# Sixteen half rows of one key transfer, loaded four rows at a time

## The chip, the core and the metric

The kernel runs on one core of a Trainium2 chip. The core has five engines that work at the same time and meet at semaphores: TensorE (PE in the profile; PEld is its loading of weights), VectorE (DVE), ScalarE (ACT), GpSimd (POOL) and SyncE (SP). Data comes from the chip's memory through 16 DMA engines, which work through queues of transfers. Here SyncE issues all transfers. The metric is the time of one execution on the device in microseconds, and the number given for a kernel is the median of its runs.

## The reference

Two layers of a decoder, each for one new token of two sequences (B = 2, D = 576). A layer is attention over a stored cache of keys and values (32 heads, 16384 positions, 128 numbers each, in bf16), and then an MLP.

```
q = (layernorm(x) @ wq) by heads                   # 2 x 32 rows of 128
p = softmax(q . K^T / sqrt(128))                    # over 16384 positions
x = x + concat(p . V) @ wo
y = layernorm(x)
x1 = y + shift(gelu(layernorm(y) @ w1)) @ w2        # shift: along a sequence of length 1
x = x + x1 + gelu(layernorm(x1) @ w3) @ w4
```

Both layers use the same caches and the same weights. K and V of one head (of one sequence) are 4 MB each, and there are 64 such heads. That is 512 MB a layer, and all of it is read once a layer, less a few heads that stay on the chip from one layer to the next.

## The kernel before, in words

**Units and places.** Heads are numbered u = 0 to 63. One tensor `mem` holds six places of 32 KB a row in 128 rows. A single head's K or V fills one place. Most heads go in pairs: K of heads u and u+1 is one block of 128 rows of 65536 bytes (names `kp`), rows 0 to 63 of the first head, the others of the second. V of a pair is loaded alike (`vp`). K of pairs alternates between two double places, V has one double place. The first layer goes through one single head, 30 pairs and three single heads; the second begins with those last three, whose K it finds on the chip, and goes on with 30 pairs and one single head.

**Transfers.** `plan_all` writes down all transfers in order, by `plan_pair`, `plan_tile` and others. Each entry has a name, a semaphore, a place and a list of starts, each with a destination and a source. `Store.pump` issues the entries strictly in this order on SyncE, each as soon as all of its place has been released, every start of an entry as a DMA of its own. An entry at the head of the list that has no place yet holds all behind it. A pair can be loaded in pieces (`cuts`, in blocks of 128 numbers of a row): pair 1 of the second layer, heads 0 and 1, comes in five, four of 8 KB a row and then the one of 32 KB a row, blocks 0 to 127. Its starts count on the semaphore `part0_0`.

**Work on a pair.** For blocks 0 to 127, `pair_transposes` (L1395) turns eight blocks at a time with TensorE, ScalarE copies them out (`evacuate`, L1496), and `pair_scores` (L1406) multiplies them with q. For blocks 128 to 255, `pair_dots` does it on VectorE (L1418, L1421). `pair_max` and `pair_exp` make the softmax, and `pair_exp` ends with a ScalarE instruction (L1460) that waits until K is no longer used; then K's place is free. In the middle of the next pair's blocks TensorE multiplies p with V (`pv_pair_part`, L1473, 256 matmuls), and ScalarE keeps the sum (`keep_pair`, L1482), after which V's place is free. The next V transfer waits for this one.

**Relays.** Landings are told to TensorE and VectorE through GpSimd (L206), which waits for the transfers' semaphores one after another in program order and counts up a semaphore of the waiting engine. `shared` and `landed` put these relays into the program.

**Between the layers.** After the last three heads come `wo`, the MLP, the second layer's `wq` (L951, L825, L843) in small transfers through a ring of places, and then the first heads of the second layer from what is on the chip (`carried`: L1506 scores, L1592 sums over V). During this the first pieces of pairs 1 and 2 of the second layer are loaded. Their issues wait for the last uses of the places.

Of the kernel before, what the change touches and what calls it, by code (L numbers as in the profile page):

```python
# [342 lines left out]
class KB:  # L343
# [117 lines left out]

        return (self.K if t == "k" else self.V)[u // self.H, u % self.H].rearrange("(p j) d -> p (j d)", p=128)

    def plan_pair(self, t, u, slot, cuts=()):

        v = (self.K if t == "kp" else self.V).rearrange("b h s d -> (b h s d)")
        n = self.NB * 128 * 128
        src = v[u * n:(u + 2) * n].rearrange("(p x) -> p x", p=128)
        for a, z in cuts or [(0, 2 * self.NB)]:
            sem = f"pair{slot}" if z - a == 2 * self.NB else f"part{slot}_{a}"  # L470
            self.store.plan((t, u, a, z - a), sem, slot * self.TILE + 256 * a, 256 * (z - a),
                            [(lambda m: m, src[:, a * 128:z * 128])])

    def plan_piece(self, t, u, base, src, a, n):
# [70 lines left out]
    def cols4(self, l, buf, m):  # L545
# [3 lines left out]
        base = 0 if buf.shape[1] == 128 * self.MT else m // half * half  # L549
        return buf[:, (lo - base) * 128 + m - lo:(hi - base) * 128:hi - lo]  # L550

    def plan_small(self, nm, l, w, at, cuts):
        D, KT, TL = self.D, self.KT, self.TL
        self.store.plan((nm, l), nm, at, 2 * KT * D, [
            ((lambda m: m[:, 0:(KT - 1) * D]), w[0:(KT - 1) * 128, :].rearrange("(p k) n -> p (k n)", p=128))] + [
            ((lambda m, a=a, b=b: m[TL + a:TL + b, (KT - 1) * D:KT * D]), w[(KT - 1) * 128 + a:(KT - 1) * 128 + b, :])
            for a, b in zip(cuts[:-1], cuts[1:])])

    def plan_all(self):

        T, U, n = self.TILE, self.U, self.KT - 1
        row, w3r, wqr = 2 * self.D, 2 * self.F, 2 * 128 * self.H
        H, MT = self.H, self.MT
        self.parts = {}
        self.plan_cols("wq", 0, self.wq, self.whole(self.wq, [4 * T, None, None, None, 4 * T + 4 * wqr]))
        self.plan_small("w2", 0, self.w2, 4 * T + wqr * n + wqr // 2, (0, 64))

        half, quarter = self.BP, self.BP // 2
        self.plan_tile("k", 0, 2)
        self.plan_tile("v", 0, 3)  # L570
        o, n = self.order(0), self.PAIRS[0]
        place = lambda i: 0 if i % 2 else 2
        self.plan_pair("kp", o[1], place(1), [(2 * half, 4 * half), (0, 2 * half)])
        for i in range(2, n + 1):
            self.plan_pair("kp", o[2 * i - 1], place(i))
            self.plan_pair("vp", o[2 * i - 3], 4)
        a, b, c = o[2 * n + 1:]
        self.plan_tile("k", a, 1)
        self.plan_tile("k", b, 0)
        self.plan_pair("vp", o[2 * n - 1], 4)  # L580
        self.plan_tile("v", a, 2)
        self.plan_tile("k", c, 3)
        self.plan_tile("v", b, 4)
        self.plan_tile("v", c, 5, self.LATE[1:-1])

        self.cuts = {}
        P = 4 * row
        ring = [3 * T - 256 * self.GONE + P * i for i in range(6)]
        assert ring[-1] + P <= 3 * T + 256 * 8 * self.PARKED
        turn = iter([ring[i] for i in (0, 2, 3, 1, 4, 5)] * 6)  # L590
        h = MT // 2
        self.cuts["wo", 0] = [(i, i + 4, next(turn)) for i in range(0, 32, 4)]
        halves = lambda n: [(k, m, z, next(turn)) for k in range(self.KT - 1) for m, z in ((0, n), (n, 2 * n))] + \
                           [(self.KT - 1, 0, 2 * n, next(turn))]
        w3 = halves(h)
        g = (0, 4, 8, 12, 16, 18)
        self.groups = [(g, g), ((0, 12, 16, 18), (0, 8, 12, 16, 18))]
        self.cuts["w4", 0] = [(h * i + p, h * i + q, next(turn)) for i in range(2) for p, q in zip(g[:-1], g[1:])]
        self.plan_rows("wo", 0, self.wo, self.cuts["wo", 0])
        self.plan_cols("w3", 0, self.w3, w3)  # L600
        self.plan_groups("w4", 0, self.w4, self.cuts["w4", 0])
        self.plan_cols("wq", 1, self.wq, halves(H // 2))

        kept = self.NB - self.GONE
        again = lambda i, z: self.plan_piece("v", U - 3, 2 * T, self.rows_of("v", U - 3), i, z - i)
        again(kept, kept + 18)
        o, n = self.order(1), self.PAIRS[1]
        early = [(2 * half + i, 2 * half + i + self.DB) for i in range(0, self.EARLY, self.DB)]
        self.plan_pair("kp", o[5], place(2), early[:1])
        again(kept + 18, self.NB - self.SPARE - self.LENT)  # L610
        self.plan_pair("kp", o[5], place(2), early[1:])
        self.plan_pair("kp", o[3], place(1), [(quarter * i, quarter * (i + 1)) for i in range(4, 8)] + [(0, 2 * half)])
        for i in range(2, n + 1):
            self.plan_pair("kp", o[2 * i + 1], place(i), [(0, 2 * half), (2 * half + self.EARLY, 4 * half)] if i == 2 else ())
            self.plan_pair("vp", o[2 * i - 1], 4)
        self.plan_tile("k", o[-1], 0)
        self.plan_tile("v", o[-1], 1)
        self.plan_pair("vp", o[2 * n + 1], 4, [(0, 2 * half), (2 * half, 4 * half)])
        at = 2 * T
        self.cuts["wo", 1] = [(i, j, at + i * row) for i, j in ((0, 32),)]  # L620
        at += 32 * row
        ats = [at, None, None, 0, w3r]
        assert at + 3 * w3r <= 4 * T
        w4_at = w3r + w3r // 2
        self.cuts["w4", 1] = [(a, b, w4_at + a * row) for a, b in ((0, 12), (12, 18), (18, 26), (26, 30), (30, 34), (34, 36))]
        w1_at = w4_at + 36 * row
        assert w1_at + 5 * row <= 2 * T
        self.plan_rows("wo", 1, self.wo, self.cuts["wo", 1])
        self.plan_cols("w3", 1, self.w3, self.whole(self.w3, ats))
        self.plan_groups("w4", 1, self.w4, self.cuts["w4", 1])  # L630
        n = self.KT - 1
        self.store.plan(("w1", 1, 0), "w1_0", w1_at, n * row, [
            (lambda m: m, self.w1[0:128 * n, :].rearrange("(p k) n -> p (k n)", p=128))])
        self.store.plan(("w1", 1, 1), "w1_1", w1_at + 4 * row, row, [(lambda m: m[self.TL:, :], self.w1[4 * 128:, :])])
# [789 lines left out]
    def halves(self):  # L1424

        return [(h, slice(64 * h, 64 * h + 64)) for h in range(2)]
# [267 lines left out]
```

## Time and profile before

| | |
|---|---|
| median of 3 runs | 2537.85 us (2537.55 to 2538.87) |
| the profiled execution | 2539.74 us, span of its instructions 2538.0 us |
| read from memory | 1090.93 MB |
| busy, PE / PEld / DVE / ACT / POOL | 64% / 58% / 74% / 49% / 1% |

The span is the time from the first to the last instruction of the profile; the execution's own time is 1.7 us longer. A share of busy time is a mean over stages with different limits. In the parts below, a number that stands behind L is a line of the kernel before. In the windows view, a DMA share or a rate counts the packets that start in a window, so in a window shorter than a packet it can be far over 1, or 0. "issue" as the end of a wait is time in which an engine waited for nothing that the profile shows.

### The profile page before, as it was taken

To read this page: it belongs to the slowest core of one execution; us is meant where nothing else is said; L and a number is where in the kernel's file an instruction comes from. 1 tells how busy PE (TensorE), PEld (TensorE's weight loads), DVE (VectorE), ACT (ScalarE), POOL (GpSimd) and SP (SyncE) were. 2 spreads that over 40 slices of the span, in tenths; PEclk is the share of its full clock that TensorE was granted. 3 is DMA by queue.
4 is the path that set the end of the run, shared out by engine and by line. 5 is a ranking of instruction groups with operands and counts; after the bars stand their busy time and mean duration, and the time that the engine had idled before them with its cause. 6 is when DMAs were issued, how large, how long until landed. Compare 5 with 4: busy or idle time off the path is not lost.

```text
span 2538.0 us, 82125 instructions
## 1 busy us (share of the span) xinstructions
PE 1626.1 (64%) x34346; PEld 1483.1 (58%) x34346; DVE 1883.8 (74%) x1559; ACT 1252.9 (49%) x1940; POOL 31.3 (1%) x95
## 2 busy tenths in 40 slices
PE   3666665666666566657767665666566566656666
PEld 3555665665566556556666655565566556555656
DVE  5877787787787777777658877877778778778773
ACT  2545545445446455455435564454554544644542
POOL 0000000000000000000000000000000000000000
PEclk8666666666666666666656666666666666666665
DMA  9999999999999999999999999999999999999999
GB/s 415 432 435 432 433 434 434 433 433 435 434 433 434 434 433 434 434 433 432 415 407 413 438 437 430 430 431 444 431 430 431 440 435 430 430 436 440 430 430 388
DMA packets 28305, 1091.78 MB, mean 430 GB/s; under 512 B 3156, under 2 KB 3288, under 8 KB 9816
## 3 DMA queue, kind: packets, MB, share of 16 engines
q1 hardware_dynamic: 28248, 1090.95, 99.8%
q8 instruction: 45, 0.74, 0.1%
q14 instruction: 12, 0.10, 0.0%
HBM read 1090.93 MB, written 0.00 MB: 430 GB/s over the span
## 4 chain that ended last, share of the span: by engine, by line
DMA 77%; PE 18%; issue 3%; ACT 2%; DVE 0%; SPq 0%; ACTq 0%; POOLq 0%; POOL 0%; DVEq 0%
DMA mem<-in_A_v_cache_dram 72%; PE mps L1473 15%; DMA mem<-in_A_wo_dram 2%; DMA mem<-in_B_w_dram 1%; DMA mem<-in_A_k_cache_dram 1%; ACT kt L1496 1%; PE mps L1592 1%; ACT o_acc L1482 0%; PE mps L951 0%; PE tps L1395 0%; DMA mem<-in_A_wq_dram 0%; PE tps L1380 0%; PE mps L1506 0%; PE tps L1506 0%; ACT both L1451 0%
## 5 line engine op out<-in xcount | busy, mean ns | idle before, releaser
L1395 PE MATMUL tps<-same,mem 128*128 128x128 bf16 x7680 | 950.5, 267 | 254.4 <-POOLq L206 252.7
L1421 DVE TENSOR_REDUCE s_dve<-prod 128x16 f32<-128x2048 bf16 x480 | 1097.4, 2286 | 16.5
L1496 ACT ACTIVATE kt<-tps 128x1024 bf16<-128x1024 bf16 x985 | 991.5, 1026 | 198.6 <-PE tps L1395 176.8
L1395 PEld LDWEIGHTS tps<-same,mem 128*128 (+1 forms) x7680 | 707.3, 112 | 364.8 <-issue 254.4
L1418 DVE TENSOR_TENSOR prod<-mem,qb 128x2048 bf16<-128x2048 bf16 x480 | 588.0, 1225 | 344.4 <-POOLq L206 280.7
L1473 PE MATMUL mps<-both,mem 128*128 128x2 bf16 x15360 | 420.1, 165 | 437.0 <-POOLq L206 423.6
L1473 PEld LDWEIGHTS mps<-both,mem 128*128 128x128 bf16 x15360 | 414.8, 103 | 442.6 <-POOLq L206 428.9
L1482 ACT ACTIVATE o_acc<-mps 128x2 f32 (+1 forms) x59 | 10.2, 173 | 794.2 <-PE mps L1473 794.2
L1406 PE MATMUL sps<-q_pair,kt 128*128 128x2 bf16 x7680 | 347.9, 167 | 50.2 <-ACT kt L1496 47.4
L1406 PEld LDWEIGHTS sps<-q_pair,kt 128*128 128x128 bf16 x7680 | 328.3, 104 | 62.0 <-ACT kt L1496 61.4
L1437 DVE TENSOR_REDUCE mq<-sps 64x1 f32<-64x128 f32 x120 | 34.6, 289 | 166.0 <-PE sps L1406 164.1
L1342 ACT ACTIVATE qb<-sps 128x128 bf16<-128x128 f32 x66 | 18.3, 277 | 139.4 <-PE sps L1338 139.4
L1338 PE MATMUL sps<-same,q_pair 128*64 128x128 bf16 x120 | 17.8, 293 | 80.3 <-DVE q_pair L1351 76.8
L1338 PEld LDWEIGHTS sps<-same,q_pair 128*64 128x64 bf16 x120 | 7.5, 121 | 85.5 <-DVE q_pair L1351 82.0
L1520 DVE TENSOR_REDUCE s_dve<-prod 128x16 f32<-128x2048 bf16 x24 | 54.9, 2286 | 0.8
L1380 PE MATMUL tps<-same,mem 128*128 128x128 bf16 x432 | 45.0, 277 | 7.3 <-POOLq L206 4.4
L1442 POOL PARTITION_ALL_REDUCE mq<-mq x60 | 21.4, 357 | 2268.8 <-DVE mq L1440 2268.8
L1451 ACT ACTIVATE both<-s_dve,mq 64x128 bf16<-64x128 f32 x120 | 47.9, 399 | 2.3
L1517 DVE TENSOR_TENSOR prod<-mem,qb 128x2048 bf16<-128x2048 bf16 x24 | 29.4, 1224 | 22.1 <-DMA mem<-in_A_k_cache_dram 12.5
L1455 ACT ACTIVATE both<-sps,mq 64x128 bf16<-64x128 f32 x120 | 43.5, 363 | 3.0
L1380 PEld LDWEIGHTS tps<-same,mem 128*128 128x128 bf16 x432 | 36.6, 127 | 8.1 <-POOLq L206 4.9
L1592 PE MATMUL mps<-p,mem 128*128 128x1 bf16 x888 | 25.8, 165 | 20.7 <-ACT p L1549 10.2
(163 smaller groups left out, 462.7 us busy)
## 6 DMA issues: line engine op xcount, KB each, us to landing
mem<-in_A_k_cache_dram SPq DMA_DIRECT2D x9, 4096.0 KB, 30.0
mem<-in_A_v_cache_dram SPq DMA_DIRECT2D x6, 4096.0 KB, 30.8
mem<-in_B_w_dram SPq DMA_DIRECT2D x23, 576.0 KB, 7.7
mem<-in_A_wq_dram SPq DMA_DIRECT2D x10, 512.0 KB, 6.5
mem<-in_A_wo_dram SPq DMA_DIRECT2D x8, 576.0 KB, 13.0
mem<-in_A_wo_dram SPq DMA_DIRECT2D x1, 4608.0 KB, 31.6
mem<-in_A_wq_dram SPq DMA_DIRECT2D x1, 4096.0 KB, 12.8
mem<-in_A_k_cache_dram SPq DMA_DIRECT2D x4, 1024.0 KB, 9.6
```

The lines of the kernel that those rows point to most:

```text
L1380: ins = pe.transpose(to[:, j * 128:(j + 1) * 128], buf[:, j * 128:(j + 1) * 128], self.ident[:, :])
L1395: ins = pe.transpose(self.tps[t][:, j * 128:(j + 1) * 128], self.mem[:, bass.ds(base + (c * self.CH + j) * 128, 128)], self.ident[:, :])
L1406: ins = pe.matmul(self.sps[1][:, i:i + 2], lhsT=buf[:, j * 128:(j + 1) * 128], rhs=self.q_pair[:, :], start=True, stop=True, skip_group_ch ...
L1418: self.dv(lambda e, base: e.tensor_tensor(out=prod, in0=self.mem[:, bass.ds(base + b * 128, DB * 128)].rearrange("p (j d) -> p j d", d=128 ...
L1421: self.dv(lambda e: e.tensor_reduce(out=self.s_dve[2][:, d * DB:(d + 1) * DB], in_=prod, axis=AX.X, op=ALU.add), reads=["prod"], writes=[( ...
L1437: self.dv(lambda e, h=h, r=r: e.tensor_reduce(out=m[r, 1:2], in_=self.pair_scored(r, h), axis=AX.X, op=ALU.max), reads=[("sps", 1)], write ...
L1451: self.act(lambda e, h=h, r=r: e.activation(out=self.both[r, h, n:2 * n], in_=self.s_dve[2][r, :], func=ACT.Exp, bias=m[r, 6:7], scale=sel ...
L1455: self.act(lambda e, h=h, r=r: e.activation(out=self.both[r, h, 0:n], in_=self.pair_scored(r, h), func=ACT.Exp, bias=m[r, 6:7], scale=self ...
L1473: ins = pe.matmul(self.mps[:, 448:450], lhsT=buf[:, at:at + 128], rhs=self.both[:, :, b], start=b == 0, stop=b == 2 * self.NB - 1, skip_gr ...
L1496: self.act(lambda e: e.activation(out=out, in_=src, func=ACT.Copy), reads=[key], writes=keys, sig=("evac", key, keys[0]))
L1520: self.dv(lambda e: e.tensor_reduce(out=self.s_dve[z][:, d * DB:(d + 1) * DB], in_=prod, axis=AX.X, op=ALU.add), reads=["prod"], writes=[( ...
L1592: ins = pe.matmul(out, lhsT=buf[:, j * 128:(j + 1) * 128], rhs=p[:, b:b + 1], start=b == 0, stop=b == self.NB - 1, skip_group_check=True)
```

## The change

`plan_pair` gets an argument `tilt`. The piece that begins at block `tilt` is no longer one transfer of 128 rows. `tilted` divides it: rows 0 to 111 as whole rows (32 KB each), the right halves of rows 112 to 127 (16 rows of 16 KB), and their left halves in four transfers of four rows (16 KB a row). It is used once, for blocks 0 to 127 of pair 1 of the second layer. All six count on the same semaphore, so whoever waits for the piece waits for all six. The bytes and their places stay the same.

```diff
-    def plan_pair(self, t, u, slot, cuts=()):
+    def plan_pair(self, t, u, slot, cuts=(), tilt=None):
...
             self.store.plan((t, u, a, z - a), sem, slot * self.TILE + 256 * a, 256 * (z - a),
+                            self.tilted(lambda m: m, src[:, a * 128:z * 128], (z - a) * 64) if a == tilt else
                             [(lambda m: m, src[:, a * 128:z * 128])])
...
+    @staticmethod
+    def tilted(to, src, cut):
+
+        lo, hi = slice(0, cut), slice(cut, src.shape[1])
+        spots = [(slice(0, 112), slice(0, src.shape[1])), (slice(112, 128), hi)]
+        spots += [(slice(p, p + 4), lo) for p in range(112, 128, 4)]
+        return [(lambda m, p=p, c=c: to(m)[p, c], src[p, c]) for p, c in spots]
...
-        self.plan_pair("kp", o[3], place(1), [(quarter * i, quarter * (i + 1)) for i in range(4, 8)] + [(0, 2 * half)])
+        self.plan_pair("kp", o[3], place(1), [(quarter * i, quarter * (i + 1)) for i in range(4, 8)] + [(0, 2 * half)], 0)
```

SyncE's transfers between the layers, before and now (rows x numbers of two bytes; the four of 128x4096 are pair 1's first pieces, 128x10240 belongs to pair 2):

```order
 L101 DMA mem<-in_A_k_cache_dram 128x2048 x2
 L101 DMA mem<-in_A_k_cache_dram 128x4096 x4
-L101 DMA mem<-in_A_k_cache_dram 128x16384 x2
+L101 DMA mem<-in_A_k_cache_dram 112x16384
+L101 DMA mem<-in_A_k_cache_dram 16x8192
+L101 DMA mem<-in_A_k_cache_dram 4x8192 x4
+L101 DMA mem<-in_A_k_cache_dram 128x16384
 L101 DMA mem<-in_A_k_cache_dram 128x10240
 L101 DMA mem<-in_A_v_cache_dram 128x32768
```

The first of the two transfers of 128x16384 has become six; the second, pair 2's, stands behind them as before. On the other four engines the instructions and their order are the same. The one wait for the piece is GpSimd's, before its first maximum of the second layer's pairs (the row with `part0_0`), and what stands around it has not moved:

```order
L1535 ISA mx<-mx 128x1 [waits piece2_84_18,piece2_102_10,part0_224,part0_192,part0_128,part0_160,done_vector]
L1286 MEMSET both 128x512
L1442 ISA mq<-mq 128x2 [waits part0_0,done_vector]
L1442 ISA mq<-mq 128x2 [waits part2_0,part2_176,part2_160,part2_128,part2_144,pair4,done_vector]
L1442 ISA mq<-mq 128x2 [waits pair0,pair4,done_vector]
```

These are the rows of before; in the changed kernel only their line numbers are nine higher.

## The prediction

> **What bounds the kernel now.** I read the page first, parts 2 to 4 and the chain of waits.
>
> ```profile
> GB/s 415 432 435 432 433 434 434 433 433 435 434 433 434 434 433 434 434 433 432 415 407 413 438 437 430 430 431 444 431 430 431 440 435 430 430 436 440 430 430 388
> ...
> q1 hardware_dynamic: 28248, 1090.95, 99.8%
> ...
> DMA 77%; PE 18%; issue 3%; ACT 2%; DVE 0%; SPq 0%; ACTq 0%; POOLq 0%; POOL 0%; DVEq 0%
> ```
>
> The 16 DMA engines are busy 99.8% of the span, at some 434 GB/s in nearly every slice, or 434 / 16 = 27.1 GB/s an engine. Every byte is loaded once, so the time is the bytes of one engine over 27.1 GB/s, plus what an engine idles, plus how far the last engine is behind the others at the end. The change leaves the bytes as they are. It can act on the other two alone. The slices below 430 (415, 407, 413, from 1206 to 1396 us) hold the passage between the layers, where the changed transfer lies. There I read the issues of the DMA queue in order of time, and from the view of DMA issues the time to landing of each.
>
> ```profile
> 1319.09 7.78 SPq L101 DMA_DIRECT2D mem<-in_A_k_cache_dram  x3
> 1344.09 0.33 SPq L101 DMA_DIRECT2D mem<-in_A_v_cache_dram  x1
> 1367.24 0.33 SPq L101 DMA_DIRECT2D mem<-in_A_k_cache_dram  x1
> 1389.95 0.33 SPq L101 DMA_DIRECT2D mem<-in_A_v_cache_dram  x1
> 1401.13 0.33 SPq L101 DMA_DIRECT2D mem<-in_A_k_cache_dram  x1
> ```
> ```profile
> mem<-in_A_k_cache_dram SPq DMA_DIRECT2D x1, 4096.0 KB, 16.7
> ...
> mem<-in_A_v_cache_dram SPq DMA_DIRECT2D x1, 28.2
> ...
> mem<-in_A_k_cache_dram SPq DMA_DIRECT2D x1, 24.6
> ```
>
> The 4096 KB issue at 1319.09 is the one that the change divides. It lands 16.7 us later, at 1335.8. The V of 1344.09 lands at 1372.3, the K of 1367.24 at 1391.8. The V of 1389.95 is issued 1.9 us before that K is in, so the queue nearly runs out. The windows view around it shows that it does (the last two columns are the busy share of the 16 DMA engines and GB/s, by packets that start in the window):
>
> ```profile
> 1387.50:1388.00 0.50, 0.50 (x23) 0.50 (x22) 0.50 (x1) 0.00 (x0) 0.00 (x0) 0.50 0.30 131
> 1388.00:1388.50 0.50, 0.50 (x25) 0.50 (x23) 0.47 (x2) 0.00 (x0) 0.00 (x0) 0.50 0.00 0
> 1388.50:1389.00 0.50, 0.50 (x25) 0.50 (x23) 0.50 (x1) 0.00 (x0) 0.00 (x0) 0.50 0.61 262
> 1389.00:1389.40 0.40, 0.40 (x22) 0.40 (x19) 0.40 (x1) 0.00 (x0) 0.00 (x0) 0.50 0.38 164
> 1389.40:1390.90 1.50, 1.50 (x30) 1.50 (x27) 1.36 (x2) 0.52 (x2) 0.00 (x0) 0.50 0.05 11
> 1390.90:1391.20 0.30, 0.30 (x6) 0.30 (x4) 0.30 (x1) 0.30 (x1) 0.00 (x0) 0.50 8.32 2840
> 1391.20:1391.50 0.30, 0.30 (x7) 0.30 (x6) 0.30 (x1) 0.30 (x1) 0.00 (x0) 0.50 1.83 655
> ...
> DMA packets 239, 13.57 MB, mean 433 GB/s; under 512 B 32, under 2 KB 32, under 8 KB 32
> ```
>
> The last row is the DMA view of a later stretch, 1420.5 to 1451.8: 207 packets over 512 B carry 13.57 MB, 65.5 KB each, which is a whole row of a pair. So a row is one packet, and a packet of 65.5 KB takes 65.5 / 27.1 = 2.42 us of its engine. Now the windows can be counted: 1 packet starts from 1387.5 to 1388.0 (131 GB/s x 0.5 us), none until 1388.5, 2 + 1 until 1389.4, then no data (16 KB of code) until 1390.9. There 13 start within 0.3 us (2840 x 0.3 / 65.5) and 3 more by 1391.5. So 13 engines were through by 1388.0 + 2.42 = 1390.4, 12 of them by 1389.9, and stood empty. Only 3 had data until 1390.9 to 1391.8. The 16 engines start again side by side at 1390.9, 0.96 us after the issue of 1389.95. **What one engine was behind another before that is mostly wiped out there.** What sets 1389.95 is TensorE, by its timeline and by SyncE's waits:
>
> ```profile
> 1343.92 2.72 PE L1395 MATMUL tps<-same,mem 128*128 128x128 bf16 x24
> ...
> 1363.93 3.26 PE L1395 MATMUL tps<-same,mem 128*128 128x128 bf16 x24
> ...
> 1377.11 1.44 PE L1473 MATMUL mps<-both,mem 128*128 128x2 bf16 x49
> ...
> 1387.39 2.25 PE L1473 MATMUL mps<-both,mem 128*128 128x2 bf16 x79 [3.74 <-issue]
> ```
> ```profile
> SPq L101 <- ACT o_acc L1482: 22.4, 1, 22.4
> ...
> PE mps L1473 <- issue: 5.3, 2, 3.7
> ```
>
> Pair 1 of the second layer starts at 1343.92, pair 2 at 1363.93; the sums over V start at 1377.11, in program order, 4.8 us after their V (1372.3). They stop twice, 5.3 us, for no data, and ScalarE's copy after them (L1482) lets the queue go on. The end shows what is at stake there: the last weight transfer is issued at 2513.65, and its landing releases the last matmuls.
>
> ```profile
> 2534.50:2535.00 0.50, 0.47 (x9) 0.23 (x5) 0.00 (x0) 0.07 (x1) 0.00 (x0) 0.50 0.08 16
> 2535.00:2535.50 0.50, 0.00 (x0) 0.00 (x0) 0.48 (x1) 0.31 (x1) 0.00 (x0) 0.50 0.06 18
> 2535.50:2536.00 0.50, 0.00 (x0) 0.00 (x0) 0.00 (x0) 0.00 (x0) 0.00 (x0) 0.50 0.05 18
> ...
> 2513.65 22.55 DMA mem<-in_B_w_dram
> ```
>
> A share of 0.06 is one engine of 16: from about 2535.0 to the landing at 2536.2 a single engine works, 1.2 us behind all others.
>
> **The change part by part.**
>
> *Issues.* One issue becomes six. An issue takes 0.33 us in the view of the issuing line:
>
> ```profile
> L101 SPq DMA_DIRECT2D mem<-in_A_k_cache_dram x74: 327/328/580, 3.1 to 2438.0; - x74
> ```
>
> Five more are 5 x 0.33 = 1.6 us, 2.9 at the slowest of the row. SyncE is then done by 1322.3; in the row of three issues that begins at 1319.09 it otherwise waits for TensorE, the last issue of that row ending at 1319.09 + 7.78 = 1326.87. The queue has work meanwhile, since the divided piece itself lands only 16.7 us after its issue. Without that cover it would be 1.6 us; with it 0.
>
> *Bytes of an engine.* 128 rows of 32 KB are 8 rows an engine, 256 KB. Now each engine gets 7 rows (112 rows) and half a row (the 16 right halves): 240 KB, 16 KB less, or 16.4 / 27.1 = 0.60 us. The left halves are 16 rows of 16 KB in four transfers. A row is one packet, so a transfer of four rows works on four engines at most. No row of before shows such a transfer, so I bound it: if they fall on all 16 engines alike, nothing changes; if all four fall on the same four engines, these have 240 + 64 = 304 KB, 48 KB more, 49.2 / 27.1 = **1.81 us later**, and the other twelve 0.60 us earlier; if all fall on a single engine, it gets 256 KB above the 240. I take the middle one, as four rows with one packet each are nearest to four engines.
>
> [...]
>
> *The waits behind it.* The landing moves from 1335.8 to between 1335.2 and 1337.6; pair 1 reads it from 1343.92, which leaves 6 us. The next K pieces, also up to 1.81 later, are read from 1363.93. V moves from 1372.3 to 1374.1 at most, against 1377.11. So TensorE and the issue at 1389.95 stay where they are; if the 4.8 us of cover were gone, the 1.81 would be paid in full.
>
> *The restart.* Twelve engines were through by 1389.9. One of these with 1.81 us more is through by 1391.7, 0.3 us after the last start seen there (1391.5, less than that for most). One of the other four ends 1.8 us later than now. The earlier ones gain nothing but idle time. From then on each engine has the same bytes as before, and the spread is carried to the end.
>
> *Sum* on the profiled execution (2539.74 us, with a span of 2538.0 and 1.7 us around it): issues 0, bytes 0 in all, TensorE 0, the four engines 0 to +0.3, of which I take +0.2: 2539.9. That execution lies 1.9 us over the median of the runs (2537.85, from 2537.55 to 2538.87); on the median, **2538.05 us**.
>
> **The rivals.**
>
> *The four engines stay last (+1.8).* If one of them is among the three that had data until 1390.9 or later, it starts V up to 1.8 us after the rest and keeps that to the end: 2539.7. For it: 3 of 16 engines were late, and four are loaded. Against it: the end is already set by a single engine 1.2 us behind, so a second engine has to pass that one first.
>
> *The end gets more even (-0.6 to -1.2).* If the engine that is last is one of the twelve and keeps its 0.60 us, or swaps its place with a loaded one, the last landing comes up to 1.2 us sooner: 2536.7. Against it: the restart lies between.
>
> *One engine takes the half rows (slower).* If the four-row transfers are not divided over engines at all, one engine carries 240 + 16 x 16 = 496 KB in place of 256; 240 KB more are 245.8 / 27.1 = 9.1 us. It ends at about 1390.4 + 9.1 = 1399.5 in place of starting V at 1390.9; V lands last on it, and the end moves by 8.6 us: 2546.4. It decides from 0.5 us of such a surplus on, which is what the empty engines had. Against it: the row-per-packet count above.
>
> *Each small transfer costs a pause (slower).* From issue to first packet the restart took 0.96 us; five more such pauses, if nothing overlapped, are 4.8 us. V would land at 1377.1, just as it is read, and the engines end at up to 1395.2 in place of 1390.9: +4.3, 2542.2. Against it stands the window from 1256 to 1290, where transfers of 576 KB follow one another:
>
> ```profile
> q1 hardware_dynamic: 3361, 13.47, 100.0%
> ...
> mem<-in_B_w_dram SPq DMA_DIRECT2D x17, 576.0 KB, 7.4
> ```
>
> with no share lost. [...]
>
> *TensorE's stops move (either sign).* Its two stops of 5.3 us before 1389.95 are not for data. If they lengthen by as much again, the restart and the end move by +5.3 to 2543.2; if they vanish, -5.3.
>
> **How the numbers follow.** A measurement of this kernel can tell about 0.2%, 5.1 us, from no change. Forecast 0.67; four engines last 0.15; a more even end 0.09; one engine 0.02; pauses 0.03, half of it past 5.1 us; TensorE's stops 0.04, half of it to each side. Faster has the 0.02 of shorter stops; slower 0.02 of one engine, 0.015 of the pauses and 0.015 of longer stops, 0.05; the rest is same, 0.93. The range starts at the lowest run less what a more even end could bring (2537.55 - 1.2 - 0.6 = 2535.75) and ends at the highest run with four engines last and the 0.3 us of the restart (2538.87 + 1.81 + 0.3 = 2541.0). The cases outside hold under 0.1.
>
> **What would show it.** Right: six issues in a row from 1319.1, with the next big K issue still about 1326; TensorE's L1395 at about 1343.9 and 1363.9; the V issue near 1390.0; windows after it in which the engines start within a microsecond of each other; the same 434 GB/s until the end. Wrong: windows near 1390 in which some engines start V two or more microseconds after the rest while the end moves with them (four engines, or one); a share under 1 between 1326 and 1340 (pauses); a V issue away from 1390 by microseconds, with TensorE's stops before it changed.

## The result and the profile after

| | before | after |
|---|---|---|
| median | 2538.01 us (6 runs, 2537.55 to 2538.87) | 2551.77 us (6 runs, 2551.36 to 2552.26) |
| the profiled execution | 2539.74 us, span 2538.0 | 2552.04 us, span 2550.2 |

The ratio is 1.0054, with a 95% interval of 1.0041 to 1.0067: 13.8 us slower. The prediction said 2538.05 us and no change, with a range up to 2541.0. It was wrong, by 13.7 us.

The page of the changed kernel, parts 2 and 4, shows where, but hardly what:

```profile
DMA  9999999999999999999999999999999999999999
GB/s 413 433 432 435 433 434 434 434 434 433 434 434 433 433 435 434 432 434 434 410 366 378 436 430 436 435 431 435 434 433 433 434 434 433 434 433 436 431 431 390
...
DMA 75%; PE 19%; issue 3%; ACT 2%; DVE 1%; SPq 0%; ACTq 0%; POOLq 0%; POOL 0%; DVEq 0%
```

Two slices of 64 us have lost speed, 407 and 413 GB/s before and 366 and 378 now, and the others are within 3% of what they were. The DMA engines are shown as busy throughout, in those slices too: they did not idle, they were slow. The windows view says how slow (the last two columns: busy share of the 16 engines, GB/s), first for the changed kernel, then for the kernel before:

```profile
1326.00:1338.00 12.00, 4.02 (x127) 3.72 (x128) 10.18 (x10) 2.49 (x5) 1.71 (x2) 0.50 1.01 242
1338.00:1350.00 12.00, 3.71 (x128) 3.54 (x127) 11.76 (x8) 1.29 (x7) 0.00 (x0) 0.50 0.99 138
1350.00:1354.00 4.00, 0.30 (x11) 0.31 (x12) 3.93 (x3) 0.00 (x0) 0.00 (x0) 0.50 0.94 389
```
```profile
1326.00:1338.00 12.00, 5.29 (x170) 4.81 (x167) 11.66 (x11) 3.56 (x12) 1.71 (x2) 0.50 1.00 429
1338.00:1350.00 12.00, 9.67 (x224) 9.59 (x225) 11.76 (x8) 5.59 (x10) 0.00 (x0) 0.56 1.01 433
```

In the first stretch the 112 rows are on their way, in the second the half rows and the four-row transfers (the fours below), with the next whole transfer behind them. With the share at 1, 242 GB/s are 15 GB/s an engine and 138 are 8.6, against 27. The bytes not moved are (429 - 242) x 12 and (433 - 138) x 12, which at 430 GB/s is 5.2 and 8.2 us. The DMA view has the same loss as the time from issue to landing:

```profile
mem<-in_A_k_cache_dram SPq DMA_DIRECT2D x1, 4096.0 KB, 35.4
...
mem<-in_A_v_cache_dram SPq DMA_DIRECT2D x1, 32.3
...
mem<-in_A_k_cache_dram SPq DMA_DIRECT2D x1, 27.6
...
mem<-in_A_v_cache_dram SPq DMA_DIRECT2D x1, 25.6
```

The first row is the whole K transfer of 4096 KB that stands behind the divided one. It is issued at about 1326 in both kernels and lands at 1361.0 where it landed at 1345.6: **15.4 us later**. This landing is what the experiments below measure. The other three are V, K and V of the next pairs, whose issues stand in SyncE's timeline:

```profile
1308.19 18.27 SPq L101 DMA_DIRECT2D mem<-in_A_k_cache_dram  x14
1354.90 0.33 SPq L101 DMA_DIRECT2D mem<-in_A_v_cache_dram  x1
1378.89 0.33 SPq L101 DMA_DIRECT2D mem<-in_A_k_cache_dram  x1
1400.28 0.33 SPq L101 DMA_DIRECT2D mem<-in_A_v_cache_dram  x1
```

V lands at 1387.2 (1372.3 before, +14.9), K at 1406.5 (1391.8, +14.7), the second V at 1425.9 (1413.1, +12.8). From there on the loss stays: the two profiled executions end 12.3 us apart, and the one before lay 1.7 us above the median of 2538.01. The 1.9 us that are won between 14.7 and 12.8 are the dry stretch in which the execution before moved 11 GB/s. V is now issued 6.2 us before K is in, and the window between the two reads

```profile
1400.30:1406.50 6.20, 3.51 (x52) 3.08 (x49) 5.51 (x4) 2.66 (x3) 0.00 (x0) 0.50 0.99 425
```

TensorE changed with it. The stop before its last matmuls over V (L1592, now L1601) was 2.2 us long in the chain of the kernel before (first fence) and is 8.8 us in the chain of the changed one:

```profile
1340.71 2.18 issue
```
```profile
1344.94 8.76 issue
...
1388.88 1.30 PE mps L1482 x49
```

So pair 1 starts 10.8 us later, and the sums over V (last row) at 1388.88, 1.7 us after their V. It was open whether this stop was a cause or came of the slow transfers. The DMA view points to the second. TensorE's stops of over 1 us that end with "issue" between 1325 and 1415, six before and seven now, all end 1.3 to 1.8 us after a packet of 16 KB of the instruction queue (q8). In the kernel before that packet ends at 1341.6 and TensorE goes on at 1342.9; in the changed kernel none starts between 1338 and 1351, and the next one ends at 1352.3, with TensorE going on at 1353.7. So the long stop fits a wait for code that came late while the loads were slow.

### The profile page after: what moved, and what is told of

Read it like the earlier page. It is cut to its first block, busy times and chain, and to the rows that moved or that the text cites. A ratio compares the mean times of both kernels' runs of the same rounds, so it can differ in the third digit from the quotient of the medians.

```text
span 2550.2 us, 82130 instructions
## 1 busy us (share of the span) xinstructions
PE 1625.9 (64%) x34346; PEld 1481.4 (58%) x34346; DVE 1883.7 (74%) x1559; ACT 1252.3 (49%) x1940; POOL 31.3 (1%) x95
## 4 chain that ended last, share of the span: by engine, by line
DMA 75%; PE 19%; issue 3%; ACT 2%; DVE 1%; SPq 0%; ACTq 0%; POOLq 0%; POOL 0%; DVEq 0%
DMA mem<-in_A_v_cache_dram 72%; PE mps L1482 16%; DMA mem<-in_B_w_dram 2%; PE mps L1601 1%; ACT kt L1505 1%; DMA mem<-in_A_k_cache_dram 1%; ACT o_acc L1491 0%; DVE s_dve L1529 0%; PE tps L1404 0%; DMA mem<-in_A_wo_dram 0%; PE tps L1389 0%; DMA mem<-in_A_wq_dram 0%; PE mps L960 0%; DVE prod L1526 0%; PE mps L1515 0%
## 5 line engine op out<-in xcount | busy, mean ns | idle before, releaser
L1601 PE MATMUL mps<-p,mem 128*128 128x1 bf16 x888 | 25.8, 165 | 29.8 <-issue 19.5
L1601 PEld LDWEIGHTS mps<-p,mem 128*128 128x128 bf16 x888 | 25.0, 104 | 30.8 <-issue 20.3
```

Of the source, the lines that this page charges most:

```text
L1601: ins = pe.matmul(out, lhsT=buf[:, j * 128:(j + 1) * 128], rhs=p[:, b:b + 1], start=b == 0, stop=b == self.NB - 1, skip_group_check=True)
```

## The experiments

Four theories stood at the start. **Pauses:** every added transfer costs the same, 15.4 / 5 = 3.1 us. **Four engines:** only the bytes of the loaded engines count, as the prediction had it. **Late code:** TensorE's long stop sets the end. **Ports** was new: the rate goes by which rows of the on-chip memory are written at the same time, and some sets of rows get in each other's way. How it sorted the rows was the author's assumption, and no run shows a rule for it. What the runs compare is sets of rows: neighbours against rows four apart, and rows 0 to 63 against 32 to 95.

All results at once. "Later" is the landing of the 4096 KB transfer behind against the kernel before (issue and DMA view of the profiled execution). The time is the difference of the medians of runs that were made together, and the last column the 95% interval of the ratio.

| run | later, us | time, us | ratio |
|---|---|---|---|
| the change | 15.4 | +13.8 | 1.0041 to 1.0067 |
| 112 + 16 whole rows | 13.0 | +12.6 | 1.0036 to 1.0063 |
| 64 + 64 rows | 12.5 | +11.5 | 1.0031 to 1.0059 |
| six by columns | -0.1 | -0.5 | 0.9989 to 1.0007 |
| fours four apart | 12.4 | +10.7 | 1.0030 to 1.0058 |
| 32 to 95 first | 7.6 | +7.5 | 1.0017 to 1.0037 |
| the same, source swapped | 11.6 | +7.6 | 1.0017 to 1.0038 |
| sixteens, neighbours | 10.5 | +9.8 | 1.0023 to 1.0050 |
| sixteens, four apart | 6.4 | +5.8 | 1.0010 to 1.0028 |
| only fours, rows 0 to 15 | -0.7 | +1.6 | 0.9995 to 1.0014 |
| only fours, rows 0 to 15, apart | -3.9 | +0.4 | 0.9992 to 1.0011 |
| only fours, 32 to 47 | -0.4 | +1.4 | 0.9994 to 1.0013 |
| only fours, 112 to 127 | 1.4 | +4.1 | 1.0007 to 1.0027 |
| only fours, 48 to 63 | 2.4 | +3.1 | 1.0005 to 1.0024 |
| only fours, 112 to 127, apart | 0.2 | +2.2 | 1.0000 to 1.0020 |
| only 112 rows | 6.9 | +5.8 | 1.0013 to 1.0033 |
| the change in another place | 16.9 (next V) | +16.1 | 1.0044 to 1.0072 |

Every edit is to the list of starts in `tilted`, but for the last row. The diffs show only the lines that tell a run from the others: `whole` is a whole row, `half` half of its length, and new `spots` stand in place of those of the change.

### Is it the number of transfers, or the rows?

Six transfers by columns:

```diff
-        spots = [(slice(0, 112), slice(0, src.shape[1])), (slice(112, 128), hi)]
-        spots += [(slice(p, p + 4), lo) for p in range(112, 128, 4)]
+        at = [0, 2048, 4096, 6144, 8192, 12288, 16384]
+        spots = [(slice(0, 128), slice(a, z)) for a, z in zip(at[:-1], at[1:])]
```

> Six transfers, all of 128 rows, cut by columns instead of rows (2048 numbers of a row four times, 4096 twice: 4 KB and 8 KB a row). As many issues and as many bytes as the change. [...] Pauses: five added transfers, 15.4 us later, time +13. Late code through six issues: TensorE's long stop comes back, time +13. Four engines: 0.

Windows, and one row of SyncE's timeline, of this kernel:

```profile
1326.00:1338.00 12.00, 7.12 (x238) 6.74 (x239) 11.79 (x10) 3.78 (x12) 1.71 (x2) 0.50 1.06 440
1338.00:1350.00 12.00, 10.63 (x213) 9.83 (x210) 11.76 (x8) 8.39 (x11) 0.00 (x0) 0.72 1.03 439
```
```profile
1384.62 0.33 SPq L101 DMA_DIRECT2D mem<-in_A_v_cache_dram  x1
```

Full speed, no loss, no time: pauses fall, and so does late code that would come of the six issues. The timeline row shows one thing more. V is issued 5.3 us earlier than in the kernel before (1389.95), because TensorE was that much earlier in this execution, and the queue does not run dry. That V lands 2.0 us sooner (1411.1 against 1413.1), and the execution takes 2538.04 us where the profiled one of the kernel before took 2539.74. The medians are 0.5 us apart, which is within the interval. So the dry stretch is not there in every execution: in the run further down that leaves this passage as it was, V is issued at 1386.93 and lands at 1411.1 too.

Two transfers of whole rows, 112 and 16:

```diff
-        spots = [(slice(0, 112), slice(0, src.shape[1])), (slice(112, 128), hi)]
-        spots += [(slice(p, p + 4), lo) for p in range(112, 128, 4)]
+        whole = slice(0, src.shape[1])
+        spots = [(slice(0, 112), whole), (slice(112, 128), whole)]
```

> 112 whole rows in one transfer and 16 whole rows in a second; no half rows and no four-row transfers. Measure: by how much the 4096 KB K transfer behind (issued at about 1326) lands later than in the kernel before, where it lands at 1345.6 (1361.0 with the change: 15.4 later), and what the run costs. [...] Pauses (each added transfer costs the same, 15.4 / 5 = 3.1 us): one added, 3.1 us later, time about +1. Four engines (only the bytes of the loaded engines count): 0, time 0. Late code (TensorE's stop of 8.8 us at 1344.9 sets the end, and comes of the six issues): 0, time 0. [...]

```profile
1326.00:1338.00 12.00, 4.09 (x136) 3.77 (x134) 9.72 (x10) 2.66 (x6) 1.71 (x2) 0.50 1.00 232
1338.00:1350.00 12.00, 3.86 (x134) 3.64 (x131) 11.79 (x7) 1.29 (x7) 0.00 (x0) 0.50 0.95 213
```

13.0 us without one half row and without one transfer of four rows: four engines falls. And two halves of 64 rows:

```diff
+        spots = [(slice(0, 64), whole), (slice(64, 128), whole)]
```

> Rows 0 to 63 in one transfer, rows 64 to 127 in a second. Same measure: the landing of the 4096 KB transfer behind. [...] Pauses: one added transfer, 3.1 us later, time about +1, as with 112 and 16 rows. Four engines: every engine has the same bytes, 0, time 0. Late code: 0, time 0.

12.5 us. After these runs a simpler theory, **half rate**, stood beside ports: any transfer of fewer than 128 rows goes at half speed, whichever rows they are. For 4.19 MB at 217 GB/s in place of 434 that is 9.7 us.

The change with its fours made of rows four apart was meant to show that the rows matter:

```diff
-        spots += [(slice(p, p + 4), lo) for p in range(112, 128, 4)]
+        spots += [(slice(112 + i, 128, 4), lo) for i in range(4)]
```

> The change, but each of its four-row transfers takes rows four apart (112, 116, 120, 124, then 113, 117 and so on) in place of four neighbours: same sizes, same counts, same bytes for each of four engines. [...] Pauses, four engines, or reading so few rows from memory at a time: as the change, 15.4 us later, time +13.8.

12.4 us, 3.0 less than the change, where pauses, four engines and few rows said the same 15.4. It spoke for ports without deciding.

### Which rows?

```diff
+        spots = [(slice(32, 96), whole), (slice(0, 32), whole), (slice(96, 128), whole)]
```

> Three transfers of whole rows: 32 to 95, then 0 to 31, then 96 to 127. Measure as before: how much later the 4096 KB transfer behind lands than in the kernel before (1345.6; two halves of 0 to 63 and 64 to 127 made it 12.5 later). [...] Half rate (any transfer of fewer than 128 rows goes at half speed, whichever rows they are; it fits both runs of two transfers, 9.7 us plus 3): 12.5 us later as the two halves, time +11.5, and rows 32 to 95 take as long as rows 0 to 63 did.

The window in which the first 64 rows are on their way, of the run of two halves (rows 0 to 63), then of this one (rows 32 to 95):

```profile
1326.00:1328.00 2.00, 0.00 (x0) 0.00 (x0) 0.04 (x1) 0.00 (x0) 0.00 (x0) 0.50 0.87 172
```
```profile
1326.00:1328.00 2.00, 0.00 (x0) 0.00 (x0) 1.83 (x3) 0.00 (x0) 0.00 (x0) 0.50 1.29 475
...
1330.00:1334.00 4.00, 2.98 (x100) 2.79 (x99) 3.93 (x6) 1.09 (x4) 0.00 (x0) 0.50 0.88 188
```

Same number of rows, same size. Rows 32 to 95 go at full speed (475 GB/s), and the transfers of 32 rows behind them at 188. Half rate falls: the landing is 7.6 us later and the time 7.5 us up, against 12.5 and 11.5 for the two halves. What remains open is the side: rows 32 to 95 were also read from other places in memory. So the source was swapped against the destination:

```diff
-        return [(lambda m, p=p, c=c: to(m)[p, c], src[p, c]) for p, c in spots]
+        spots = [(slice(32, 96), slice(0, 64)), (slice(0, 32), slice(64, 96)), (slice(96, 128), slice(96, 128))]
+        return [(lambda m, p=p: to(m)[p, whole], src[s, whole]) for p, s in spots]
```

> Which side makes it slow, the memory that is read or the rows that are written? Rows 0 to 63 of the source are written to rows 32 to 95, source rows 64 to 95 to rows 0 to 31, and 96 to 127 to themselves: what is read first is what the run of two halves read first (slow there), where it is written is where the run of 32 to 95 wrote first (full speed there). With it K of this half piece stands in the wrong rows, so the values of this pair are others; the work is the same. Ports (the written side): as the run of 32 to 95, 7.6 us later, time +6.5 to +8, first transfer at full speed (packets of 32 KB at 1.2 us). Memory side: first transfer at half speed (2.4 us), 10 to 12.5 us later, time +10 to +12.

```profile
1326.00:1328.00 2.00, 1.72 (x65) 1.63 (x62) 1.97 (x2) 0.17 (x1) 0.00 (x0) 0.50 0.98 422
```

The source rows that went at 172 GB/s into rows 0 to 63 go at 422 into rows 32 to 95. It is the written side. (This profiled execution, 2549.82 us, was the slowest of its kernel, and the piece ahead of the divided one already landed 1.7 us late in it, which is in the 11.6; another 2.3 us above the run before it are not traced. The median of its runs is 7.6 us up, as ports said.)

Eight transfers of 16 rows, neighbours or four apart, grade it further:

```diff
+        half = src.shape[1] // 2
+        spots = [(slice(0, 128), slice(half, 2 * half))] + [(slice(p, p + 16), slice(0, half)) for p in range(0, 128, 16)]
```

> The right half of all 128 rows in one transfer, the left half in eight transfers of 16 neighbouring rows (16 KB of a row each, one row an engine). [...] Half rate: the left half takes twice its 4.8 us, 4.8 to 8 us later, time +3 to +7.

```diff
+        spots += [(slice(p + i, p + 64, 4), slice(0, half)) for p in (0, 64) for i in range(4)]
```

> As the run of sixteens, with the same number of transfers of the same size, but the 16 rows of one are four apart (0, 4, ... 60, then 1, 5, ... and so on, then from 64). [...] Half rate: the same as with neighbours, 4.8 to 8 us.

Windows of the neighbours, then of the rows four apart:

```profile
1330.00:1336.00 6.00, 2.94 (x98) 2.80 (x99) 5.90 (x7) 0.81 (x4) 1.71 (x2) 0.50 0.96 153
```
```profile
1330.00:1336.00 6.00, 3.05 (x103) 2.82 (x101) 5.90 (x7) 1.15 (x4) 1.71 (x2) 0.50 1.01 221
```

Rows four apart give 221 GB/s, half of 434 within 2%, and a landing 6.4 us later; neighbours give 153 and 10.5. Transfers and bytes are the same in both, so the 4.1 us between them come of the rows. Half rate had both at 4.8 to 8 us.

### Where it is put

```diff
-            ... [(quarter * i, quarter * (i + 1)) for i in range(4, 8)] + [(0, 2 * half)], 0)
+            ... [(0, 2 * half), (2 * half, 4 * half)] if i in (15, 16) else (), 0 if i == 15 else None)
```

> The same six transfers in another place: on the first half of K of pair 15 of the second layer, where the queue never runs dry; the passage between the layers is as before. (K of pairs 15 and 16 is loaded in two halves of 128 rows there, so that the half can be divided.) Ports or half rate, the engines being the bound: the loss of 15.4 us is paid in full, with no 2 us of idle to take it from: time +14 to +16. If the loss hung on the passage between the layers (code loads, TensorE's stops there): 0 to +5.

SyncE's timeline of the kernel before, then of this run, and this run's windows:

```profile
1807.70 0.33 SPq L101 DMA_DIRECT2D mem<-in_A_v_cache_dram  x1
...
1885.11 0.33 SPq L101 DMA_DIRECT2D mem<-in_A_v_cache_dram  x1
```
```profile
1805.55 0.33 SPq L101 DMA_DIRECT2D mem<-in_A_v_cache_dram  x1
...
1899.86 0.33 SPq L101 DMA_DIRECT2D mem<-in_A_v_cache_dram  x1
```
```profile
1834.00:1850.00 16.00, 10.92 (x323) 10.87 (x323) 13.18 (x9) 3.10 (x4) 0.00 (x0) 0.53 0.96 212
1850.00:1862.00 12.00, 2.01 (x34) 1.42 (x32) 1.06 (x5) 5.12 (x16) 0.35 (x1) 0.61 0.96 130
```

The same two steps, 212 and 130 GB/s, far from the passage between the layers. The run is 2.15 us ahead of the kernel before at the one V and 14.75 behind at the other: 16.9 us, and 16.1 in the time, as nothing is there to take it from. Neither TensorE's stops nor the passage are needed for the loss, so the 8.8 us stop was a consequence or at most a part, not the cause.

### What each part costs

To price each part alone, the left half was loaded for 16 rows only (`lo`, `hi` as in the change), first rows 0 to 15 as four times four neighbours:

```diff
+        spots = [(slice(0, 128), hi)] + [(slice(p, p + 4), lo) for p in range(0, 16, 4)]
```

> The four-row transfers by themselves: the right half of all 128 rows in one transfer, then the left half of rows 0 to 15 alone in four transfers of four neighbouring rows, on four engines. The left half of rows 16 to 127 is left out (1.8 MB less), so what is left saves 4.8 us before the fours are counted. [...] Pauses: 4 x 3.1 - 4.8 = 7.6 us later.

Then the same rows and bytes, each transfer with rows four apart (0, 4, 8, 12, then 1, 5, 9, 13 and so on):

```diff
+        spots = [(slice(0, 128), hi)] + [(slice(i, i + 16, 4), lo) for i in range(4)]
```

> [...] Pauses, or four rows being few: as with neighbours.

The stretch of the fours in the windows of the first and of the second:

```profile
1330.00:1334.00 4.00, 3.06 (x103) 2.84 (x101) 3.93 (x6) 1.17 (x4) 0.26 (x1) 0.50 1.09 369
```
```profile
1330.00:1334.00 4.00, 3.10 (x104) 2.94 (x105) 3.93 (x3) 1.56 (x5) 0.00 (x0) 0.50 1.06 451
```

With rows four apart the fours cost little but their bytes: 451 GB/s and the earliest landing of all, 3.9 us before the kernel's, where the 1.84 MB left out are 4.2. With neighbours the rate is 369 GB/s: 32 KB take an engine 1.55 us in the mean of that window (1.09 x 16 x 4 us over 369 x 4 / 32.8 packets) in place of 1.2. The change itself had shown 138 GB/s in this step. No view names the engine of a packet, but that the same four engines carry all four transfers shows in the packets of the changed kernel. Of its 32 packets of 16 KB on the queue of the loads that start from 1337 to 1349 (16 half rows and the 16 rows of the fours), 20 stand in four chains of five, in which each starts within 0.03 us of the end of the last; one chain starts at 1338.86, 1340.43, 1343.29, 1345.49 and 1348.09. The other twelve stand alone. The landings of the two runs were 3.2 us apart. The second run tells one thing more: it lands 3.9 us earlier than the kernel and is no faster, as the V behind it is issued at 1389.44, hardly sooner than 1389.95.

The change's fours are on rows 112 to 127. So the same transfers were put there, then on 48 to 63, and on 112 to 127 four apart:

```diff
+        spots = [(slice(0, 128), hi)] + [(slice(p, p + 4), lo) for p in range(112, 128, 4)]
```

> As the run of the fours by themselves (right half of 128 rows, then four transfers of four neighbours of the left half), but on rows 112 to 127, where the change has them, in place of rows 0 to 15; the left half of rows 0 to 111 is left out. [...] That the fours need the 112 and 16 rows ahead of them to be slow: as on rows 0 to 15, 320 to 420 GB/s and no later than the kernel.

```diff
+        spots = [(slice(0, 128), hi)] + [(slice(p, p + 4), lo) for p in range(48, 64, 4)]
```

> [...]

```diff
+        spots = [(slice(0, 128), hi)] + [(slice(112 + i, 128, 4), lo) for i in range(4)]
```

> [...]

The same window of the three, in this order:

```profile
1330.00:1334.00 4.00, 2.94 (x98) 2.80 (x99) 3.93 (x6) 0.99 (x4) 0.23 (x1) 0.50 0.99 147
```
```profile
1330.00:1334.00 4.00, 3.25 (x106) 3.05 (x107) 3.93 (x6) 1.38 (x4) 0.00 (x0) 0.50 0.95 135
```
```profile
1330.00:1334.00 4.00, 2.94 (x98) 2.80 (x99) 3.93 (x6) 0.86 (x4) 0.00 (x0) 0.50 0.98 221
```

The fours are slow here without the 112 and 16 rows ahead of them. Four engines that carry the fours, at 27.1 GB/s at the most, bring all sixteen down to 147, 135 and 221 GB/s, with a busy share of 0.95 to 0.99. The other twelve alone could send 12 x 27.1 = 325. And in the first of the three windows 32 KB take an engine 3.5 us in the mean (0.99 x 16 x 4 us over 147 x 4 / 32.8 packets) in place of 1.2; in the changed kernel the packets of 32 KB that start from 1339 to 1346 take 3.8 to 5.2 us. So engines that carry none of the fours are held up too, with the fours in either half of the rows. What holds them up is not shown. The landings are 1.4, 2.4 and 0.2 us later than the kernel's.

Once more, on rows 32 to 47:

```diff
+        spots = [(slice(0, 128), hi)] + [(slice(p, p + 4), lo) for p in range(32, 48, 4)]
```

> The fours by themselves once more (right half of 128 rows, then four transfers of four neighbours of the left half; the rest of the left half is left out), on rows 32 to 47. [...]

```profile
1330.00:1334.00 4.00, 3.10 (x105) 2.88 (x103) 3.93 (x6) 1.21 (x4) 0.13 (x1) 0.50 1.05 291
1328.00:1334.00 6.00, 4.02 (x127) 3.72 (x128) 5.90 (x7) 2.49 (x5) 0.13 (x1) 0.50 0.96 262
```

The landing, 0.4 before the kernel's, is near that of rows 0 to 15 (0.7 before). The rate lies between: 291 GB/s from 1330 to 1334, and 262 from 1328 on, where rows 0 to 15 have 352, rows 112 to 127 186 and rows 48 to 63 194. So it matters which sixteen neighbours are written; what tells the faster sets from the slower ones is not shown. Last, the 112 rows alone:

```diff
+        spots = [(slice(0, 112), slice(0, src.shape[1]))]
```

> [...]

```profile
1326.00:1338.00 12.00, 4.02 (x127) 3.72 (x128) 9.34 (x10) 2.49 (x5) 1.71 (x2) 0.50 1.00 251
```

6.9 us later, with 16 rows (0.52 MB, 1.2 us) fewer: the 112 rows cost 8.1 us of the change's 15.4.

## Why the prediction was wrong

**The step that failed is "Bytes of an engine".** It counted the bytes of each engine and priced every one of them at 27.1 GB/s, whatever rows they go to. The rate came from rows of the trace in which every transfer has 128 rows, and no row showed another. Its extremes (nothing, 1.81 us on four engines, all on one) only varied which engine carries the bytes. What the runs showed in its place is that the rate depends on the rows: 434 GB/s in transfers of 128 rows, 242 in the stretch of the 112 rows, 221 and 153 with sixteens four apart and of neighbours, 147 and 135 with the fours on rows 112 to 127 and 48 to 63. The transfer that had been priced as free, 112 rows at seven an engine, cost 8.1 us. The fours and half rows, priced at 1.81, cost the other 7.3 (15.4 - 8.1). Even the 16 rows alone cost more than 1.81: the run of 112 + 16 less the 112 alone is 13.0 - 6.9 = 6.1 us, 1.2 of them bytes.

**Issues:** right. The row of fourteen issues ends at 1326.5 (1308.19 + 18.27), and the row of before, with five fewer, at 1326.9; six transfers by columns cost nothing.

**The waits behind it:** the frame was right, the numbers fell with the step above. A landing between 1335.2 and 1337.6 was inside the 6 us that TensorE leaves; with 138 GB/s until 1350, it is outside. Of the 4.8 us ahead of the sums over V 1.7 were left, and TensorE's own stop grew from 2.2 to 8.8 us.

**The restart:** right for the execution that it was read from, and it is why the loss shrank from 14.7 to 12.8 us between K's and V's landings. But that execution lay 1.7 us above the median, and two others pass the same place with next to no dry stretch (V issued at 1384.62 and 1386.93), so it could not be counted on. It holds to the other side too: 3.9 us gained before it (the fours on rows 0 to 15, four apart) bought no time, since V's issue hangs on TensorE.

**The rivals.** *Four engines stay last* and *a more even end* drown in the loss. *One engine takes the half rows* (2546.4) and *each small transfer costs a pause* (2542.2) lay on the right side by wrong mechanisms: 112 + 16 whole rows have no half rows and lose 13.0 us; six transfers by columns lose nothing, and nine with sixteens lose 5.8 us with rows four apart and 9.8 with neighbours. Five added transfers of 512 and 1024 KB in a filled queue left 440 GB/s, and with four of 64 KB on rows 0 to 15, four apart, the rate stayed at 451. *TensorE's stops move:* the two stops that it names went from 5.3 to 4.0 us (1.33 and 2.65); those that grew lie before pair 1 (1.4 and 2.2 to 4.2 and 8.8), as a consequence. Where V was issued 5.3 us earlier, V landed 2.0 us sooner and the execution was 1.7 us shorter, so this rival had its gain too large.

**Why the range did not hold it.** It had no term for the written side at all. "128 rows" stood in every transfer of the trace; the one thing that the change does is to leave that form, and the rate was carried over all the same.

## What to carry to other kernels

A rate read from a trace belongs to the form of the transfers it was read from: before cutting a load by rows, ask for each piece which rows of the on-chip memory it writes, and measure its rate. Cutting by columns with all 128 rows kept cost nothing here (six pieces, 440 GB/s); of the cuts by rows, 64 rows from 32 to 95 ran at full speed (475 GB/s in their window) where 0 to 63 ran at 172. A busy share of 1 in the DMA rows says nothing on speed (0.99 stood beside 138 GB/s, 1.01 beside 433), so read it with the GB/s beside it.

## What was not expected of the hardware

- Engines that carry none of the small transfers are slowed as well: four transfers of 64 KB, on four engines, held all sixteen to 147 and 135 GB/s on rows 112 to 127 and 48 to 63. On rows 0 to 15 and 32 to 47 the same transfers left 369 and 291 GB/s. Why the other engines are held up, and why so much less in the second case, is not settled.
- 112 rows in one transfer, with 16 engines at work, move at 242 to 251 GB/s, little over half of what 128 rows do.
- The times of the runs with the fours on rows 112 to 127, neighbours and four apart, and on rows 48 to 63 lie 0.7 to 2.7 us above their landings. Where that rest comes from stays open.
- TensorE's stops for no data end 1.3 to 1.8 us after a packet of 16 KB of the instruction queue, in the kernel before and in the changed one. In the changed kernel none of these packets starts between 1338 and 1351, with the loads at 138 GB/s from 1338 to 1350, and the stop there is 8.8 us: long stops of TensorE can come with slow loads and not be their cause.
